# Linear attention and a maxout layer on one core: tiles of two pairs, held loads, maxima by block transposes, a new table

## The chip, the cores and the metric

The kernel runs on one core of a Trainium2 chip. The metric is the device time of one launch in microseconds (us). Three runs of the kernel before gave 290.2, 291.66 and 295.25 us; their median, 291.66 us, is the time before.

## The reference

Eight batches with eight heads each of 576 positions and 64 channels go through an attention with an exponential feature map, and the result goes through a maxout layer.

```python
def phi(x):
    proj = einsum('bhsd,df->bhsf', x, w_phi)                  # 64 -> 128 features
    proj = proj - max(abs(proj), axis=-1, keepdims=True)
    return concatenate([exp(proj), exp(-proj)], axis=-1)
q_p, k_p = phi(q), phi(k)
kv = einsum('bhsf,bhsd->bhfd', k_p, v)
z = sum(k_p, axis=2)
num = einsum('bhsf,bhfd->bhsd', q_p, kv)
den = einsum('bhsf,bhf->bhs', q_p, z)[..., None] + 1e-06
x = (num / den), heads side by side: 4608 tokens x 512
h = maximum(maximum(x @ w1, x @ w2), x @ w3)                   # 512 -> 768
out = h @ w_out                                                # 768 -> 512
```

## The kernel before

**Units and chunks.** The 64 heads are worked in 16 units of four heads, two pairs each (`attention(u)`). After two units one batch is complete, and `chunk(b, ...)` puts its first 512 positions through the maxout layer; the last 64 positions of all batches form chunk 8. The maxout is computed as w1 plus two maxima of differences, so a chunk has products "up" and "up2" (54 groups of each in all, four products of 512 columns a group, L700) and products "straight" and "down" into the output (L728, L733). The weights w2 - w1 and w3 - w1 are made by GpSimd and VectorE (L771), and w1 times w_out by TensorE once (transposes L783, products L797).

**One unit.** Tiles of 128 positions (two heads of 64) have q in partitions 0 to 63 and k in 64 to 127. Units 0 to 3 are brought into this form by TensorE transposes (L483, then a VectorE copy L486), the later ones by a DMA transpose (L498). Unit 0's q and k come in float32 through SyncE's queue in four loads, each of one pair of q or k (L441), and are cast (L445); units 1 to 3 come through GpSimd's software queue, which casts on the way (L452); the later ones come in float32 and are cast by GpSimd (L469). Products with w_phi follow (L521): for each tile one product for q on the upper 64 rows of the array and one for k on the lower 64 rows, side by side, in five groups of four or two tiles, into the banks psq and psk. VectorE takes the maxima of absolute values of both (L540), ScalarE the exponentials of k (L534).

The maxima of q have to be subtracted from the projections of q that have features in partitions. In units 0 and 1 that is done by products of the maxima with the negative identity (L602, L605). In the other 14 units TensorE transposes the maxima (L548), VectorE or ScalarE copies them (L552), and one DMA puts them into row 64 of the tiles (L556), over k, which has been used by then; one product of 65 rows on the whole array, with the weights `wphi_m` whose row 64 is -1, then gives the projection less the maximum (L600, five groups of 512, 512, 512, 512 and 256 columns). ScalarE takes both exponentials (L613). GpSimd scales v by the factors of k (em, L571, L575). 72 products of 64 rows, again side by side, form kv (L629), 40 products form numerator and denominator (L647), VectorE divides (L653, L654), and the unit's result is turned by TensorE (units 0 and 1, L667) or by a DMA transpose (L677).

**The order.** Every piece of work is a node. The order of all nodes, their engine and their PSUM bank or buffer are written out in a table, `PLAN`; a word like `15T1@5.6` says that node 15 goes to TensorE with bank 1, and is due at 5.6 us. Nothing waits for a due time: each engine runs its nodes in the order of the table, and waits only for the data and buffers that it needs. The due times come from a planner's costs, which are also written in the node (`{"PE": 0.87}`). The order binds within each engine's queue, GpSimd's and SyncE's queues of DMA issues among them. `fill` puts idle products (L828) where the table leaves gaps on TensorE.

```python
GROUPS = [(0, 4), (4, 4), (9, 4), (13, 4), (8, 2)]
a = nd("G", {"PE": 0.12 if n == 2 else 0.236 * len(part)}, ...)   # projections
a = nd("M", {"PE": 0.22 if n == 4 else 0.12}, mm, [n_v, n_phi], [qkT, psm, Eqb])
```

## Time and profile before

| what | value |
|---|---|
| median of three runs | 291.66 us |
| time of the profiled execution | 291.96 us |
| span of its profile, first to last instruction | 290.1 us |
| mean granted TensorE clock | 0.988 |
| TensorE busy (matmul) | 274.1 us |
| VectorE busy | 203.6 us |
| ScalarE busy | 199.4 us |
| GpSimd busy | 117.2 us |
| idle products of `fill` (L828) | 7.7 us |

The span is one profiled execution; 1.86 us lie outside it in the profiled time. A group of instructions in the page has a line of the kernel, an engine, an operation, the tiles it writes and reads, a count, the busy time and the mean of one. Matmuls are pipelined, so a product's own duration (379 ns for 512 columns) is longer than the step from its start to the next one's (0.22 us), and how long TensorE really takes for a group is read from starts. A busy share is a share of the stretch named; what a stage is bound by is read from the stretch, not from the whole.

### The profile page before, as it was taken

The page shows a single profiled execution, that of the slowest core. Times are in us where ns is not written, and L with a number is a line of the kernel's source. Part 1 is how long each engine was busy: PE and PEld are TensorE (multiplying, and loading weights), DVE is VectorE, ACT ScalarE, POOL GpSimd, SP SyncE. Part 2 cuts the span into 40 slices and gives each one's busy share as a digit, 9 for nine tenths or more (in the row PEclk, how much of TensorE's full clock was granted, in tenths as well). Part 3 has the DMA queues.
Part 4 walks back from the last instruction along what each step waited for, and adds up shares of the span by engine and source line. Part 5 has one row for each costly group of instructions (what it writes and reads, how often), then busy time and mean ns, then how long its engine had stood idle before and what let it go on. Part 6 is the DMA issues. An engine that isn't in the chain of part 4 may idle for free.

```text
span 290.1 us, 8530 instructions
## 1 busy us (share of the span) xinstructions
PE 274.1 (94%) x3526; PEld 154.6 (53%) x3563; DVE 203.6 (70%) x433; ACT 199.4 (69%) x455; POOL 117.2 (40%) x102
## 2 busy tenths in 40 slices
PE   8579989999999898999999999999999999999995
PEld 3347566455555554655556466465544654444443
DVE  3578898999898887797789869996673342156300
ACT  2579897899999877986797887889758420341021
POOL 8044889385746345836184535060606000000000
PEclk9897999999999999999999999999999999999999
DMA  7999979999998899999999991994620006370055
GB/s 173 276 251 209 283 157 263 231 281 217 226 186 307 169 273 197 291 276 241 205 263 224 274 285 35 163 183 87 144 49 0 2 3 127 70 168 18 0 129 163
DMA packets 68273, 51.48 MB, mean 177 GB/s; under 512 B 48778, under 2 KB 53002, under 8 KB 68234
## 3 DMA queue, kind: packets, MB, share of 16 engines
q1 hardware_dynamic: 63759, 45.55, 66.2%
q0 software_dynamic: 4000, 4.92, 9.8%
q8 instruction: 28, 0.46, 0.6%
q10 hardware_dynamic: 475, 0.46, 0.5%
q14 instruction: 11, 0.09, 0.1%
HBM read 34.67 MB, written 9.44 MB: 152 GB/s over the span
## 4 chain that ended last, share of the span: by engine, by line
PE 84%; DMA 10%; DVE 3%; issue 1%; POOL 1%; ACT 0%; POOLq 0%; DVEq 0%
PE ups L700 32%; PE ops L733 15%; PE ops L728 9%; PE psn L647 6%; PE kvps L629 6%; DMA w_bf<-in_moe_w_dram 6%; PE psq L521 5%; PE psm L600 5%; DMA xT<-x_sb 2%; DMA qkT<-mT 2%; PE pm L797 1%; PE tps L483 1%; DVE x_sb L654 1%; PE psm L602 1%; POOL qk_bf L452 1%
## 5 line engine op out<-in xcount | busy, mean ns | idle before, releaser
L700 PE MATMUL ups<-xT,w_bf 128*128 128x512 bf16 x414 | 100.5, 379 | 2.1 <-DMA xT<-x_sb 1.2
L534 ACT ACTIVATE Ek<-psk 128x512 bf16<-128x512 f32 (+1 forms) x160 | 81.6, 567 | 13.3 <-PE psk L521 6.9
L575 POOL TENSOR_TENSOR vab<-v_raw,em 128x1152 bf16<-128x1152 f32 (+1 forms) x36 | 68.2, 1907 | 49.8 <-ACT em L571 35.7
L613 ACT ACTIVATE Eq<-psm 128x512 bf16<-128x512 f32 (+1 forms) x160 | 80.2, 576 | 8.5 <-PE psm L600 7.3
L700 PEld LDWEIGHTS <-w_bf 128*128 128x128 bf16 x432 | 40.2, 98 | 45.9 <-issue 1.3
L540 DVE TENSOR_REDUCE mqp<-psq 128x4 bf16<-128x512 f32 (+1 forms) x80 | 48.9, 633 | 6.8 <-PE psk L521 5.9
L706 DVE TENSOR_TENSOR hT<-hT,ups 128x512 bf16<-128x512 bf16 x54 | 36.1, 682 | 24.0 <-PE ups L700 18.1
L540 DVE TENSOR_REDUCE mk<-psk 128x4 f32<-128x512 f32 (+1 forms) x80 | 49.3, 630 | 3.1 <-PE psk L521 1.7
L733 PE MATMUL ops<-wout_bf,hT 128*128 128x512 bf16 (+1 forms) x216 | 51.0, 373 | 0.4 <-issue 0.2
L741 ACT COPY osb<-ops 128x512 f32<-128x512 f32 (+1 forms) x24 | 13.7, 578 | 33.9 <-PE ops L733 27.4
L654 DVE TENSOR_TENSOR x_sb<-psn,rden 128x320 bf16<-128x320 f32 x64 | 31.5, 492 | 2.2
L733 PEld LDWEIGHTS <-hT 128*128 128x128 bf16 x222 | 21.0, 98 | 22.1
L708 ACT ACTIVATE hT<-ups 128x512 bf16<-128x512 f32 x36 | 21.7, 609 | 14.5 <-PE ups L700 13.6
L647 PEld LDWEIGHTS <-Eq 128*128 128x128 bf16 x640 | 25.4, 97 | 9.2
L647 PE MATMUL psn<-kv_sb,Eq 128*128 128x65 bf16 x640 | 27.8, 194 | 0.1
L521 PE MATMUL psq<-w,qkT 64*128 64x128 bf16 x288 | 25.3, 223 | 1.4 <-DVE qkT L486 0.7
L521 PE MATMUL psk<-w,qkT 64*128 64x128 bf16 x288 | 25.3, 224 | 0.0
L521 PEld LDWEIGHTS <-qkT 64*128 64x128 bf16 x576 | 17.1, 96 | 14.0 <-issue 10.4
L728 PE MATMUL ops<-xT 128*128 128x512 bf16 x88 | 24.1, 379 | 0.4
L600 PE MATMUL psm<-qkT,wphi_m 128*128 128x512 bf16 (+1 forms) x70 | 21.7, 358 | 1.4 <-DVE hT L706 0.8
L741 DVE COPY osb<-ops 128x512 f32<-128x512 f32 x13 | 8.9, 686 | 18.9 <-PE ops L733 16.1
L469 POOL CAST qk_bf<-k_raw 128x1152 bf16<-128x1152 f32 x12 | 14.1, 1185 | 18.2 <-DMA k_raw<-in_k_dram 13.0
(70 smaller groups left out, 232.0 us busy)
## 6 DMA issues: line engine op xcount, KB each, us to landing
v_raw<-in_v_dram SPq DMA_DIRECT2D x16, 576.0 KB, 5.2
out_dram<-osb SPq DMA_DIRECT2D x65, 128.0 KB, 2.5
q_raw<-in_q_dram SPq DMA_DIRECT2D x12, 576.0 KB
k_raw<-in_k_dram SPq DMA_DIRECT2D x12, 576.0 KB, 5.1
w_bf<-in_moe_w_dram POOLq DMA_DIRECT2D x3, 768.0 KB, 12.5
qk_bf<-in_k_dram POOLq DMA_DIRECT2D x3, 288.0 KB, 16.2
qk_bf<-in_q_dram POOLq DMA_DIRECT2D x3, 288.0 KB, 12.0
wout_bf<-in_moe_w_out_dram POOLq DMA_DIRECT2D x1, 768.0 KB, 21.1
```

Of the source, the lines that this page charges most:

```text
L521: nc.tensor.matmul(ps()[:, i, :], lhsT=cols[r, :], rhs=w2[r, c, :], start=True, stop=True)
L534: nc.scalar.activation(Ek[s]()[:, tiles_of(t0, n), :], of(1), EXP, scale=1.0 - 2.0 * s)
L540: nc.vector.tensor_reduce((mq, mk)[c]()[:, tiles_of(t0, n)], of(c), AXX, ALU.max, apply_absolute_value=True)
L575: (nc.vector if n_.eng == "DVE" else nc.gpsimd).tensor_tensor(vab()[:, g, t0:t1, 0:D], vb()[:, t0:t1, :], em()[:, g, t0:t1].unsqueeze(2).t ...
L600: nc.tensor.matmul(psm()[:, 0:w], lhsT=wphi_m, rhs=rhs, start=True, stop=True)
L613: nc.scalar.activation(Eqb()[s][:, cols], psm()[:, 0:w], EXP, scale=1.0 - 2.0 * s)
L647: nc.tensor.matmul(psn()[:, c, :], lhsT=Eqb()[g][:, t0:t0 + P], rhs=kv()[:, pr, ab, g, :], start=(g == 0), stop=(g == 1))
L654: nc.vector.tensor_tensor(x_sb()[:, pr, :, ab, :], psn()[:, :, 0:D], rden().to_broadcast([P, 5, D]), ALU.mult)
L700: nc.tensor.matmul(ups(), lhsT=w_bf[i + 1][:, ct, j * P:(j + 1) * P], rhs=tokens_of(ct), start=(ct == 0), stop=(ct == CT - 1))
L706: nc.vector.tensor_tensor(hT()[:, j, :], hT()[:, j, :], ups(), ALU.max)
L728: nc.tensor.matmul(ops_()[:, 0:width], lhsT=tile_of(ct, tt), rhs=line_w[c_i > MOVE][:, ct, cols], start=(ct == 0), stop=False)
L733: nc.tensor.matmul(ops_()[:, 0:width], lhsT=hT()[:, j, tt * P:(tt + 1) * P], rhs=wout_bf[:, j, cols], start=False, stop=(j == JT - 1))
```

## The change

Six things change together.

- **Tiles.** A tile now has one kind alone, q or k, with one pair of heads in partitions 0 to 63 and the other in 64 to 127. The two products of a tile, one on each half of the array's rows, go to two banks and belong to the two pairs. The five groups are: k and q tiles 0 to 3, k and q tiles 4 to 7, and tile 8 of both; the reductions and exponentials of the last group come in four pieces of 128 columns each instead of two of 256. For unit 0, where both pairs lie side by side in the cast copy, one transpose of 128 x 128 makes a tile instead of two.
- **Subtraction of the maxima.** VectorE turns the maxima by four 32 x 32 transposes, with no TensorE transpose and no copy out of PSUM. Two DMAs instead of one put them into rows 0 and 64 of the k tiles. The products of q are then two on each half: one with `w2`, one with `less`, whose rows 0 and 64 are -1 and whose other rows are zero. They are issued in two nodes per unit instead of five, the ninth tiles' products before the others of the first node and behind them in the second, and the second node's wait on a semaphore for the first node's.
- **Loads.** Unit 0's q and k come in pieces of four and five tiles of both pairs instead of one pair each, in the order k 4 to 8, q 4 to 8, k 0 to 3, q 0 to 3. GpSimd issues w1 first and unit 1's q behind it, and its next load, unit 1's k, waits behind a one-element copy that needs the first tiles of unit 0's q; all further GpSimd work stands behind it in its queue.
- **Groups of two.** The products of two banks can be split into halves that run side by side (`side_by_side`). The list `HALVED` chooses this for one group alone, numerator and denominator of the second pairs of unit 11; all others stay in full.
- **Nodes.** up, up2, straight and down come in pairs with the same products as before.
- **Table.** All 1498 nodes have a new place, 27 instead of 18 of the first maxout evacuations (L710) lie on VectorE, and all 28 DMAs of maxima are issued by SyncE (13 of 14 before).

```diff
--- before.py
+++ after.py
-GROUPS = [(0, 4), (4, 4), (9, 4), (13, 4), (8, 2)]
-BATCHES = [(0, 8), (9, 8), (8, 2)]
+GROUPS = [(1, 0, 4), (0, 0, 4), (1, 4, 4), (0, 4, 4), (None, 8, 1)]
+BATCHES = [(0, 0, 8), (1, 0, 8), (None, 8, 1)]
+FIRST = 1
+PIECES = [(1, 0, 4), (0, 0, 4), (1, 4, 4), (0, 4, 4), (None, 8, 1)]
 EW = UT * P + D
+TURN = 0.3
+TQ = 32
...
-2D0@0.8 4A@2.0 0G@0.5 6S0@0.7 3D@1.1 10S0@1.3 11D0@5.0 5D@5.5 7A@4.2 15T1@5.6 16D0@6.4 86D0@7.2 26T002300@7.2 29D@7.6 8S@1.9
...
+2D0@0.8 3D@1.1 12S0@0.7 13D0@4.2 8S0@1.2 9D@5.0 4A@2.0 5D@5.5 0G@0.5 19T1@4.9 23T2@5.7 24D0@6.2 21T3@5.8 20A@5.4
+35T004500@6.4 22D@6.5 45T67@6.6 47D@6.9 46D@7.2 10S@1.7 11A@6.0 15T1@6.8 16D@7.4 42T23@7.1 43D@7.7 6S@2.2 7A@6.6 17T1@7.9
...
+HALVED = """
+00000000000000000000000100000000000000000000000000000000000000000000000000000000000000000000000000000000000
...
+    ROWS = (slice(0, D), slice(D, P))
+
+    rows_done = tc.alloc_semaphore("rows_done")
+    turns = [0]
+
+    def half_full(ins):
+
+        turns[0] += 1
+        ins.then_inc(rows_done, 1)
+        tc.add_to_no_dep_group(f"turn{turns[0]}", ins.ins)
+        tc.no_tile_sem_insts.add(ins.ins.name)
+        return turns[0]
+
+    def behind(turn, product):
+
+        if not turn:
+            return product()
+        nc.tensor.wait_ge(rows_done, turn)
+        ins = product()
+        tc.declare_fence(ins.ins, group=f"turn{turn}")
+        return ins
+
+    halved, n_groups = [c == "1" for c in HALVED if c in "01"], [0]
+
+    def new_group():
+
+        n_groups[0] += 1
+        return n_groups[0] - 1, halved[n_groups[0] - 1]
+
+    def in_full(ps, steps, opens, closes):
+
+        for n, step in enumerate(steps):
+            out_, lhsT, rhs = step(ps, slice(0, P))
+            nc.tensor.matmul(out_, lhsT=lhsT, rhs=rhs, start=opens and n == 0, stop=closes and n == len(steps) - 1)
+
+    def side_by_side(state, steps, opens, closes, turn=None, turns_after=True):
+
+        for n, step in enumerate(steps):
+            for half in ((0, 1), (1, 0))[state]:
+                i = half ^ state
+                out_, lhsT, rhs = step(i, ROWS[half])
+                ins = behind(turn, lambda: nc.tensor.matmul(out_, lhsT=lhsT, rhs=rhs, start=opens and n == 0,
+                                                            stop=closes and n == len(steps) - 1))
+                turn = None
+        return half_full(ins) if turns_after and not closes else None
...
-    w2 = const.tile([P, 2, DF], BF16, name="w2")
-    wphi_m = const.tile([P, DF], BF16, name="wphi_m")
+    w2 = const.tile([P, DF], BF16, name="w2")
+    less = const.tile([P, DF], BF16, name="less")
...
+        nc.vector.memset(less, 0.0)
+        for p0 in (0, D):
+            nc.vector.memset(less[p0:p0 + 1, :], -1.0)
...
+            if what < 2 and u == 0:
                 mains.append(None)
+                for c0, c1 in ((0, 4), (4, NT)):
+                    def main(what=what, c0=c0, c1=c1, raw=raw):
+                        nc.sync.dma_start(by_pairs(raw())[:, :, c0 * D:c1 * D], rows_of(what, 0, 0, 2)[:, :, c0 * D:c1 * D])
+                    n_ = nd("const", {"SP": 0.5}, main, [], [raw], pipe=1.6 * (c1 - c0) / NT, lat=1.7, packet=PACKET)
+
+                    def to_bf16(n_, what=what, c0=c0, c1=c1, raw=raw):
+                        copy_on[n_.eng](half_of(what, c0, c1), by_pair(raw())[:, :, c0:c1, :])
+                    n_ = nd("C", {"DVE": 0.1 + 0.09 * (c1 - c0), "ACT": 0.2 + 0.1 * (c1 - c0)}, None, [n_], [raw, qk])
+                    n_.fn = lambda n_=n_, f=to_bf16: f(n_)
+                    cast.append((what, c0, c1, n_))
+            elif what < 2 and by_pe:
+                mains.append(None)
+
+                def main(what=what):
+                    nc.gpsimd.dma_start(by_pairs(qk()[:, what]), rows_of(what, u, 0, 2))
+                deps = []
+                if u == 1 and what == FIRST:
+                    deps = [nd("gate", {"POOL": 0.1}, lambda: nc.gpsimd.tensor_copy(
+                        qk()[0:1, FIRST, 0, 0:1], raw_bufs(0)[0]()[0:1, 0, 0:1]), [n_ for w_, c0, c1, n_ in units[0]["loads"] if w_ == 0 and c0 == 0],
+                        [raw_bufs(0)[0], qk])]
+                cast.append((what, 0, NT, nd("L", {"POOL": 0.85}, main, deps, [qk], pipe=1.8, lat=2.1, packet=PACKET_BF)))
...
+                def tp(tiles=tiles, tps=tps):
+                    for i, (w_, c) in enumerate(tiles):
+                        if not raw_form:
+                            nc.tensor.transpose(tps()[:, i, :], qk()[:, w_ * NT + c, :], ident)
+                            continue
+                        for pr in range(2):
+                            nc.tensor.transpose(tps()[ROWS[pr], i, :], qk()[:, w_, pr * NT + c, :], ident)
...
+        for what, c0, n in GROUPS:
+            ps = [bank("psp", [P, 4, DF]) for _ in range(2)]
+            tail = what is None
+
+
+            def proj(what=what, c0=c0, n=n, ps=ps, tail=tail):
+                for i in range(2 if tail else n):
+                    for half in range(2):
+                        t = i * NT + c0 if tail else what * NT + c0 + i
+                        nc.tensor.matmul(ps[half]()[:, i, :], lhsT=qkT()[ROWS[half], t * P:(t + 1) * P], rhs=w2[ROWS[half], :],
+                                         start=True, stop=True)
+            a = nd("G", {"PE": 0.11 if tail else 0.22}, proj, [tr[x] for x in tiles_of(what, c0, n)] + [n_phi],
+                   [qkT, mk, mq] + ps + Ek, mode=1)
+            if what != 0:
+                projs.append(a)
+            for w_, i in [(w_, i) for w_ in ((0, 1) if tail else (what,)) for i in range(2)]:
+                to = slice(i * NT + c0, i * NT + c0 + n)
+                of = slice(w_, w_ + 1) if tail else slice(0, n)
+
+                def red(w_=w_, i=i, to=to, of=of, ps=ps):
+                    nc.vector.tensor_reduce((mq, mk)[w_]()[:, to], ps[i]()[:, of, :], AXX, ALU.max, apply_absolute_value=True)
+
+                def ex(s, i=i, to=to, of=of, ps=ps):
+                    nc.scalar.activation(Ek[s]()[:, to, :], ps[i]()[:, of, :], EXP, scale=1.0 - 2.0 * s)
+                for s in range(2 if w_ else 0):
+                    exps.append(nd("ek", {"ACT": 0.49 if n == 4 else 0.24}, lambda s=s, ex=ex: ex(s), [a],
+                                   [ps[i], Ek[s]], locks=[ps[i]]))
+                n_ = nd("r", {"DVE": 0.607 if n == 4 else 0.22}, red, [a, n_const], [ps[i], (mq, mk)[w_]], locks=[ps[i]])
+                reds[w_].append((n_, (i,)))
...
-            pmT = bank("pmT", [P, P], BF16)
-            n_r = nd("R", {"PE": 0.06}, lambda: nc.tensor.transpose(pmT(), mq(), ident), reds[0::2], [mq, pmT])
-            mT = buf("mT", 2, [UT, P], BF16)
-
-            def do_mT(n_):
-                copy_on[n_.eng](mT(), pmT()[0:UT, :])
-            n_mt = nd("mT", {"ACT": 0.25, "DVE": 0.2}, None, [n_r], [pmT, mT], locks=[pmT])
-            n_mt.fn = lambda: do_mT(n_mt)
-            n_v = nd("V", {"ACT": 0.7, "SP": 0.7}, None, [n_mt] + projs, [mT, qkT], lat=2.2, pipe=0.1)
-            n_v.fn = lambda: queue_of[n_v.eng].dma_start(
-                qkT()[D:D + 1, :].rearrange("o (t c) -> o t c", c=P), mT())
+            mT = buf("mT", 2, [TQ, P + TQ], BF16)
+
+            def across():
+                for g in range(P // TQ):
+                    nc.vector.transpose(mT()[:, g * TQ:(g + 1) * TQ], mq()[g * TQ:(g + 1) * TQ, :])
+            n_r = nd("R", {"DVE": 0.35}, across, q_reds, [mq, mT])
+            n_v = []
+            for pr in range(2):
+                def row(n_, pr=pr):
+                    queue_of[n_.eng].dma_start(qkT()[pr * D:pr * D + 1, NT * P:UT * P].rearrange("o (c i) -> o c i", i=P),
+                                               mT()[pr * NT:(pr + 1) * NT, 0:P])
+                n_ = nd("V", {"ACT": 0.65, "SP": 0.6}, None, [n_r] + projs, [mT, qkT], lat=2.2, pipe=0.1)
+                n_.fn = lambda n_=n_, f=row: f(n_)
+                n_v.append(n_)
...
-                    nc.tensor.matmul(psm()[:, 0:w], lhsT=wphi_m, rhs=rhs, start=True, stop=True)
...
+        eqs = {}
+        pst, done, a = bank("psm", [P, 2, P]), {}, None
+        for ab in range(2):
+            ch = ROWS[ab]
+            psm = [bank("psm", [P, 8, D]) for _ in range(2)]
+
+            def mm(ab=ab, ch=ch, psm=psm):
+                def main(w, t0, pr, **kw):
+                    return nc.tensor.matmul(psm[pr](), lhsT=w[ROWS[pr], :], rhs=tiled(qkT())[ROWS[pr], t0:t0 + NT - 1, ch], **kw)
+
+                def last(w, t, start, stop):
+                    kw = dict(start=start and not ab, stop=stop and bool(ab))
+                    return nc.tensor.matmul(pst()[:, ab, :], lhsT=w[ROWS[ab], :], rhs=tiled(qkT())[ROWS[ab], t, :], **kw)
+                parts = ((w2, 0, dict(start=True, stop=False)), (less, NT, dict(start=False, stop=True)))[0:2 - by_product]
+                for w, t0, kw in parts if not ab else ():
+                    ins = last(w, t0 + NT - 1, **kw)
+                if not ab:
+                    done[0] = half_full(ins)
+                for w, t0, kw in parts:
+                    for pr in ((0, 1), (1, 0))[ab]:
+                        main(w, t0, pr, **kw)
+                turn = done[0]
+                for w, t0, kw in parts if ab else ():
+                    behind(turn, lambda: last(w, t0 + NT - 1, **kw))
+                    turn = None
+                if by_product:
+                    for pr in range(2):
+                        for c in range(NT - 1):
+                            nc.tensor.matmul(psm[pr]()[:, c, :], lhsT=mq()[:, pr * NT + c:pr * NT + c + 1].to_broadcast([P, P]),
+                                             rhs=minus[:, ch], start=False, stop=c == NT - 2)
+                    for pr in range(2 * ab):
+                        nc.tensor.matmul(pst()[:, pr, :], lhsT=mq()[:, pr * NT + NT - 1:(pr + 1) * NT].to_broadcast([P, P]),
+                                         rhs=minus, start=False, stop=pr == 1)
+            cost = (0.49, 0.49) if not by_product else (0.86, 0.98)
+            a = nd("M", {"PE": cost[ab]}, mm, [n_phi] + (q_reds + [n_minus] if by_product else n_v) + ([a] if a else []),
+                   [qkT, Eqb, pst] + psm + ([mq] if by_product else []), mode=1)
...
+            psn, done = [bank("psn", [P, 5, W]) for _ in range(2)], {}
+
+            g_, half = new_group()
+
+            def nmm(state, pr=pr, psn=psn, done=done, half=half):
+                def step(c, g):
+                    def of(ab, r):
+                        t0 = (8 * pr + 4 * ab + c if c < 4 else MT + pr) * P + (D if c == 4 and ab else 0)
+                        return psn[ab]()[:, c, :], Eqb()[g][r, t0:t0 + P], kv()[r, pr, ab, g, :]
+                    return of
+                if half:
+                    done[state] = side_by_side(state, [step(c, g) for c in range(5) for g in range(2)], not state, bool(state), done.get(0))
+                else:
+                    for c in range(5):
+                        in_full(state, [step(c, g) for g in range(2)], True, True)
+            two = []
+            for state in range(2):
+                two.append(nd("N", {"PE": 0.3 if half else 0.312}, lambda state=state, f=nmm: f(state),
+                              (two if half else []) + (n_kvs if half else [n_kvs[state]]) + (eqs[pr, 0] + eqs[pr, 1] if half else eqs[pr, state])
+                              + eqs[False], [Eqb, kv, x_sb] + (psn if half else [psn[state]]), mode=int(half),
+                              hold=TURN if half and state else None, group=g_))
```

642 lines of the change are left out of this document (307 added, 335 removed).

## Prediction

> **What bounds the kernel now.** I read the busy times first, then the same by stretches of the span, then the starts of single products on TensorE, last the waits and the shapes on VectorE.
>
> ```profile
> PE 274.1 (94%) x3526; PEld 154.6 (53%) x3563; DVE 203.6 (70%) x433; ACT 199.4 (69%) x455; POOL 117.2 (40%) x102
> PEclk9897999999999999999999999999999999999999
> ```
>
> TensorE is busy nearly all the time at full clock, except at the start. By stretches (busy us of each engine, count in brackets, then clock, DMA share, GB/s):
>
> ```profile
> 10.00:20.00 10.00, 7.77 (x116) 4.48 (x116) 7.88 (x15) 8.77 (x20) 1.97 (x3) 0.83 1.13 272
> 20.00:30.00 10.00, 9.21 (x191) 7.15 (x193) 7.70 (x14) 8.00 (x21) 5.25 (x7) 0.83 1.21 208
> 30.00:110.00 80.00, 76.42 (x1223) 45.27 (x1233) 72.14 (x157) 70.69 (x166) 51.77 (x41) 1.00 0.99 237
> 110.00:215.00 105.00, 102.55 (x1421) 59.11 (x1437) 85.83 (x184) 86.54 (x200) 46.65 (x34) 1.00 0.88 198
> 215.00:290.00 75.00, 71.36 (x538) 35.83 (x543) 26.48 (x50) 22.82 (x48) 5.62 (x6) 1.00 0.28 66
> ```
>
> From 30 us on TensorE idles 9.6 of 260 us, and the last 3.6 of these are mostly the tail. So a microsecond of work added to TensorE there is nearly a microsecond of time, and one taken away likewise. VectorE is at 90% between 30 and 110 us, ScalarE at 88%: room, but little. Before 30 us TensorE waits for loads:
>
> ```profile
> PE tps L483 <- ACT qk_bf L445: 2.5, 2, 1.3
> PE pwT L783 <- DMA w_bf<-in_moe_w_dram: 1.8, 1, 1.8
> ```
>
> Unit 0's second halves of q and k are cast only at 8.71 and 10.26 us, and w1 lands at 20.57. Everything below is added to the profiled execution, 291.96 us (span 290.1), which lies 0.3 above the median 291.66. A measurement can tell about 2% (5.8 us) from no change.
>
> **TensorE, products.** The view of starts shows what a product of half the rows costs, and what a change between half and full rows costs.
>
> ```profile
> 119.97 0.22 PE L521 MATMUL psq<-w,qkT 64*128 64x128 bf16 x1
> 119.97 0.22 PE L521 MATMUL psk<-w,qkT 64*128 64x128 bf16 x1
> 120.03 0.22 PE L521 MATMUL psq<-w,qkT 64*128 64x128 bf16 x1
> 120.03 0.22 PE L521 MATMUL psk<-w,qkT 64*128 64x128 bf16 x1
> 120.18 2.76 PE L700 MATMUL ups<-xT,w_bf 128*128 128x512 bf16 x12
> 122.88 0.23 PE L521 MATMUL psq<-w,qkT 64*128 64x128 bf16 x1
> ```
>
> A pair of half products starts together and is followed by the next pair 0.06 us later. After the last pair the next product, on all rows, starts 0.15 us later: 0.10 lost. I took all such changes after 30 us, from start to start, less the columns at 128 in 0.053 us: 33 into half rows lose 0.099 in the median, 33 out of them 0.095, while 210 changes between groups of full rows lose 0.003. Now the orders: with the projections and kv as the only half groups the old table has 65 changes after the start stage (66 are in the trace). In the new one the subtraction is a half group as well, and with the one halved group there are 96. 31 x 0.10 = **+3.1 us**.
>
> The subtraction's columns: before 4 x 512 + 256 = 2304 a unit on all rows, 0.96 us. After, two products for each 512, side by side in pairs: 4 x 2 x 512 / 2 = 2048 columns of time, plus the ninth tiles, 2 x 2 x 128, on one half alone. If products start in order, as the pairs above do, nothing runs beside these 512 and a unit takes 1.07 us, 0.107 more; if the other half runs past them, 0.96 and nothing. 14 units: 0 to +1.5; I take **+1.5**, since every start in the view is in order. The Trainium skill, page TensorEngine Tiling (Array Packing), section Key Properties, says that tiles operate independently; by that the term would be 0 and the sum 294.3. The trace shows independence only for neighbours in order.
>
> The transpose of the maxima goes: 14 x 0.06 (start 41.67, next product 41.73) = **-0.8**. The projections (36 products a unit), kv, divisions and the maxout groups keep their products: 0. The halved group has as many columns in pairs; its wait for its own first half, and the like wait in each second subtraction node, stand in TensorE's queue ahead of all later products: 0 for the latter, as eight half products lie between, at most the 0.22 of one product's duration for the former. In units 0 and 1 the subtraction loses columns, and unit 0 loses 18 transposes (about 0.5 us); both lie where TensorE waits anyway: 0, or -1.
>
> **VectorE and ScalarE.** Rows by shape:
>
> ```profile
> L540 DVE TENSOR_REDUCE mqp<-psq 128x4 bf16<-128x512 f32 x64 | 42.8, 686 | 6.5 <-PE psk L521 5.6 <-PE psq L521 0.5
> L540 DVE TENSOR_REDUCE mqp<-psq 128x2 bf16<-128x256 f32 x16 | 6.8, 422 | 0.4 <-PE psk L521 0.4
> L552 DVE COPY mT<-pmT 18x128 bf16<-18x128 bf16 x8 | 1.6, 206 | 1.9 <-PE pmT L548 1.9
> ```
>
> From 512 to 256 columns a reduction loses 0.264 us, so one of 128 costs about 0.29, or 0.23 behind another (neighbours overlap by some 0.055). 64 x 0.23 in place of 32 x 0.37 is +2.9. Four 32 x 32 transposes do not occur before; VectorE's smallest rows are 0.11 (memset) to 0.21 (the copy above), less overlap 0.055 to 0.155, so 14 x 4 gives 3.1 to 8.7; I take 0.13, near the 1x1 cast (0.135), +7.3. The copies save 1.6; nine more maxout evacuations at 0.63 add 5.7, and take 5 from ScalarE, to which 64 short exponentials in place of 32 add about as much (0.404 for 256 columns, 0.61 for 512). VectorE in sum: +14, from 10 to 16. About 6 of it fall between 30 and 110 us: 72.1 + 6 = 78 of 80. The fullest 10 us now hold 9.84 (50 to 60 us), so VectorE becomes level with TensorE there. I charge **+1.5**: 78 at 96% need 81.5 us. The bounds are 0 (other engines' waits give way) and the second rival below.
>
> **DMA queues.** SyncE issues 28 DMAs of maxima for 13, at 0.81 us each now (0.78 to 1.08); 14 more cost it some 9 us, hidden as SyncE mostly waits (single waits up to 28 us). Behind them stand loads and transposing DMAs; without cover a unit's tiles come 0.7 later. The bytes stay.
>
> **Start.** GpSimd's first five issues now stand between 1.42 and 6 us. The packets show that its software queue works in order, from 4.0 us on, and that it shares with SyncE's one to one: 387 to 383 packets between 4 and 10 us. After the change w1 and unit 1's q fill that queue at once, so the held loads (unit 1's k, unit 2, w_out) would not have run earlier anyway, and unit 0's last piece still comes near 10.3: before it 1180 KB have to pass, about 600 of them after 4 us. Behind GpSimd's wait stand these loads and its work on v; none is needed before about 18 us. What changes is w1: first in the queue, its 512 packets of 0.134 us, alternating with pieces of 1 to 1.3 KB (0.047 for 1 KB), end near 10.5 instead of 20.6. The wait of 1.8 us goes; next late is unit 0's q. I take **-1.5**; bounds -4.3 (both waits above) and +1 (q later, since the pieces have half the bytes and the rival packets are larger).
>
> **Sum:** 291.96 + 3.1 + 1.5 - 0.8 + 1.5 - 1.5 = 295.8 us, 1.4% above the median. With the terms at their bounds (6.9 for VectorE, from the second rival): 289.0 to 303.7.
>
> **Rivals.**
> - *The hold does nothing.* The start term is then 0, as w1 only changes places with q and k of unit 1 and something else is late: 297.3. For it: one to one sharing. The Trainium skill, page DMA: Bandwidth & Descriptors, section Queues, rings and completion order, has each engine go round between rows packet by packet; then one load in GpSimd's queue takes the same turns as six, and the trace agrees (387 to 383). Against it: w1's place.
> - *VectorE becomes the bound.* It is at 90% between 30 and 110 us and never over 98%. If 90% is all that this order of waits allows, 78.4 us need 86.9: +6.9 for +1.5, 301.2. It decides once VectorE's added work in that stretch exceeds 0.9 x 80 - 72, which is nothing. For it: 9.6 us of VectorE's idle time end with a reduction, most of them waits for products, so the two engines wait for each other. Against it: 50 to 60 us.
> - *Unit 1's k is late.* The hold opens near 10.5, issue 0.8. The first software load now takes 7.0 us to its last packet (18.3), w1 17.0. The order wants it at about 19.4 (due 15.9, and the start runs 3.5 late). If it takes 10.7, everything moves by 2.6: 298.4. Decides beyond 8 us.
> - *Faster.* The order of waits improves with w1 early and TensorE's idle between 30 and 110 us (3.6) goes; changes of rows hide in waits of others: 291.96 - 0.8 - 4.3 - 3.6 = 283.3. For it: the clock was halved twice (0.83 in two stretches) and w1's wait lies ahead of the second. Against it: TensorE's work rises.
>
> **Numbers.** Forecast 0.36, hold without effect 0.10 (both within 2%, 0.46); VectorE 0.26 and late k 0.12 (slower, 0.38); faster 0.16. The range from 286.5 to 302 leaves out most of the fast case (about 0.12) and the top of the slow one (0.08).
>
> **What would show it.** Changes of rows: starts of the new subtraction products 0.15 behind a full product; span of TensorE after 30 us. Subtraction: 1.07 or 0.96 us a unit. VectorE: 0.13 for a transpose, over 95% between 30 and 110 us. Start: no wait of L783 for w1, first exponentials still near 10.8 us. I am wrong if TensorE gains idle time beyond 12 us after 30, or if the first kv comes over 3 us earlier or later than 28.0.

## The result and the profile after

The changed kernel takes 298.88 us in the median of four runs (297.9 to 300.0) where the kernel before takes 291.69: ratio 1.027, 95% interval 1.020 to 1.033. A second measurement, beside runs 5 and 6 below, gave 299.8 against 290.4 us, ratio 1.031 (1.026 to 1.036). So it is slower by 2.5 to 3%; I use 1.029, the middle of the two, to compare with. (Ratios leave out executions that took over 1.5% longer than the fastest of the same kernel; in the third move of run 7 these are three of six, so its median and its ratio do not match.) The profiled execution is 298.36 us long, span 296.6, 6.4 more than the one before.

From the page of the changed kernel, the busy times and the granted clock in 40 slices:

```profile
PE 279.2 (94%) x3658; PEld 157.3 (53%) x3658; DVE 220.8 (74%) x524; ACT 195.7 (66%) x470; POOL 117.7 (40%) x104
PEclk9879999999999999999999999999999999999999
```

TensorE is as full as before in sum. VectorE has gained 17.2 us, of which 9.0 lie behind 215 us, where it has room: it is busy there for 35.45 of 81.6 us, for 26.48 of 75 before. The view by stretches of the changed kernel (busy us of PE, PEld, DVE, ACT and POOL, then clock, DMA share, GB/s):

```profile
10.00:20.00 10.00, 7.40 (x77) 4.58 (x77) 5.37 (x12) 7.35 (x18) 3.47 (x6) 0.66 1.10 200
20.00:30.00 10.00, 8.87 (x217) 6.36 (x215) 9.91 (x22) 10.00 (x29) 7.81 (x11) 1.00 0.84 162
30.00:110.00 80.00, 74.10 (x1225) 44.02 (x1222) 74.60 (x181) 67.76 (x170) 49.46 (x39) 1.00 1.00 243
40.00:64.00 24.00, 18.88 (x275) 10.68 (x275) 21.51 (x47) 17.40 (x44) 21.05 (x15) 1.00 0.88 243
110.00:215.00 105.00, 103.85 (x1499) 59.01 (x1498) 91.27 (x226) 86.68 (x212) 47.47 (x35) 1.00 0.86 197
```

Two things differ from before. Between 30 and 110 us TensorE is busy for 74.1 us, 2.3 fewer than before, and more than all of that lies between 40 and 64 us: 18.9 there, where the kernel before has this:

```profile
40.00:64.00 24.00, 22.55 (x295) 12.88 (x297) 22.29 (x47) 20.50 (x49) 17.68 (x12) 1.00 0.86 238
```

And from 110 to 215 us TensorE is full (103.85 of 105). The waits of TensorE in the changed kernel say what opened the hole (total, times, longest; the first row lies in the start):

```profile
PE tps L547 <- ACT qk_bf L501: 4.4, 2, 2.8
PE kvps L710 <- POOL vab L641: 2.2, 2, 1.9
PE ups L381 <- DVE mqp L597: 1.4, 1, 1.4
```

The wait for w1 is gone, as forecast. A wait for GpSimd's multiplication of unit 2's v (L641) is new; so is one for VectorE's maxima (near 59 us). The chain of the changed kernel leads from that wait back to a load (start, length):

```profile
34.37 0.05 DVE v_raw L519
...
34.44 8.46 DMA v_raw<-in_v_dram
...
43.04 0.11 POOL vab L641
43.15 1.97 issue
45.12 2.13 POOL vab L641
...
47.29 1.24 PE kvps L710 x70
...
57.37 2.18 DVE w_bf L900
59.55 0.61 DVE mqp L597
```

VectorE's gate copy (a one-element copy that the load waits for) ran at 34.4 us, behind reductions and divisions in VectorE's queue. Unit 2's load of v took 8.5 us, GpSimd's two multiplications 4.2 (the "issue" of 1.97 is the first of them), and TensorE stood from 45.4 to 47.3. From 48.7 to 62.8 us the chain runs through VectorE alone, and 5.0 us of it are the three differences of weights (L900).

How the loss builds up is seen best against the table: the lag of an instruction is its start less its due time. The median over all reductions, exponentials, divisions and maxout evacuations due in ten microseconds:

| due from | before | changed | difference |
|---|---|---|---|
| 30 us | 6.5 | 5.7 | -0.8 |
| 40 us | 8.3 | 8.9 | 0.7 |
| 60 us | 8.9 | 12.2 | 3.3 |
| 150 us | 11.9 | 15.8 | 3.9 |
| 250 us | 12.2 | 16.6 | 4.4 |

The new table itself ends 2.1 us later (its last TensorE node at 276.45 against 274.35), and 2.1 + 4.4 are the 6.5 us of the span. A start that is 0.8 better is followed by 4.1 us lost between 30 and 60 us, and by a slow leak of 1.1 us after that. In the second profiled execution of the changed kernel the lag is 6.3 us at 30, 12.5 at 60 and 16.8 at 250: the start is only 0.3 better there, and 3.8 us are lost between 30 and 60 us.

### The profile page after: what moved, and what is told of

It reads as the page before. It is cut to its first block, busy times and chain, and to the rows that moved or that the text cites. A ratio compares the mean times of both kernels' runs of the same rounds, so it can differ in the third digit from the quotient of the medians.

```text
span 296.6 us, 8888 instructions
## 1 busy us (share of the span) xinstructions
PE 279.2 (94%) x3658; PEld 157.3 (53%) x3658; DVE 220.8 (74%) x524; ACT 195.7 (66%) x470; POOL 117.7 (40%) x104
## 4 chain that ended last, share of the span: by engine, by line
PE 71%; DVE 12%; DMA 10%; ACT 3%; issue 1%; POOL 1%; SPq 0%; DVEq 0%; POOLq 0%
PE ups L381 28%; PE ops L381 23%; PE kvps L710 5%; PE psn L381 5%; PE psp L586 4%; DMA xT<-x_sb 4%; PE psm L662 4%; DVE mqp L597 3%; DMA q_raw<-in_q_dram 3%; DVE mk L597 3%; DMA v_raw<-in_v_dram 3%; DVE w_bf L900 2%; ACT Ek L600 1%; ACT Eq L694 1%; DVE qkT L553 1%
## 5 line engine op out<-in xcount | busy, mean ns | idle before, releaser
L600 ACT ACTIVATE Ek<-psp 128x512 bf16<-128x512 f32 (+1 forms) x192 | 83.5, 520 | 11.8 <-PE psp L586 7.0
L641 POOL TENSOR_TENSOR vab<-v_raw,em 128x1152 bf16<-128x1152 f32 (+1 forms) x36 | 68.5, 1918 | 43.9 <-ACT em L637 29.3
L694 ACT ACTIVATE Eq<-psm 128x512 bf16<-128x512 f32 (+1 forms) x160 | 77.3, 584 | 5.8 <-PE psm L662 4.7
L597 DVE TENSOR_REDUCE mqp<-psp 128x4 bf16<-128x512 f32 (+1 forms) x96 | 50.0, 551 | 8.9 <-PE psp L586 6.6
L597 DVE TENSOR_REDUCE mk<-psp 128x4 f32<-128x512 f32 (+1 forms) x96 | 49.8, 547 | 7.2 <-ACT Ek L600 4.1
L809 DVE TENSOR_TENSOR hT<-hT,ups 128x512 bf16<-128x512 bf16 x54 | 35.7, 682 | 11.5 <-PE ups L381 9.8
L811 ACT ACTIVATE hT<-ups 128x512 bf16<-128x512 f32 x27 | 16.0, 614 | 21.3 <-PE ups L381 21.1
L586 PE MATMUL psp<-w,qkT 64*128 64x128 bf16 x576 | 27.0, 220 | 1.5 <-DVE qkT L553 0.9
L586 PEld LDWEIGHTS <-qkT 64*128 64x128 bf16 x576 | 18.2, 95 | 17.0 <-issue 11.5
L813 DVE TENSOR_SCALAR hT<-ups 128x512 bf16<-128x512 f32 x27 | 18.3, 685 | 7.1 <-PE ups L381 7.1
L710 PE MATMUL kvps<-vab,Ek 64*128 64x65 bf16 x1152 | 20.6, 190 | 2.6 <-POOL vab L641 2.2
L870 DVE COPY osb<-ops 128x512 f32<-128x512 f32 (+1 forms) x14 | 8.7, 628 | 18.9 <-PE ops L381 14.6
L710 PEld LDWEIGHTS <-Ek 64*128 64x128 bf16 x1152 | 19.1, 94 | 5.3 <-issue 3.2
## 6 DMA issues: line engine op xcount, KB each, us to landing
w_bf<-in_moe_w_dram POOLq DMA_DIRECT2D x3, 768.0 KB, 12.5
```

Of the source, the lines that this page charges most:

```text
L586: nc.tensor.matmul(ps[half]()[:, i, :], lhsT=qkT()[ROWS[half], t * P:(t + 1) * P], rhs=w2[ROWS[half], :], start=True, stop=True)
L597: nc.vector.tensor_reduce((mq, mk)[w_]()[:, to], ps[i]()[:, of, :], AXX, ALU.max, apply_absolute_value=True)
L600: nc.scalar.activation(Ek[s]()[:, to, :], ps[i]()[:, of, :], EXP, scale=1.0 - 2.0 * s)
L641: (nc.vector if n_.eng == "DVE" else nc.gpsimd).tensor_tensor(vab()[:, g, t0:t1, 0:D], vb()[:, t0:t1, :], em()[:, g, t0:t1].unsqueeze(2).t ...
L694: nc.scalar.activation(Eqb()[s][:, to:to + w], ps().rearrange("p a b -> p (a b)"), EXP, scale=1.0 - 2.0 * s)
L710: nc.tensor.matmul(kvps[ab]()[:, t // NT, g, :], lhsT=Ek[g]()[r, t, :], rhs=vab()[r, g, t, :], start=(t + g == 0), stop=(t == UT - 1 and g ...
```

## The experiments

Three theories. A: VectorE's added work is what comes back in the time. B: the hole from 45 to 47 us, with what feeds it, does. C: the added changes between half and full rows do, all along the span. Some edits change a due time in the table and leave the word where it is: the program sorts the nodes by their due times before it issues them, so that the due time sets the place in an engine's queue.

**1. No hold.** The copy that holds GpSimd's queue does nothing.

```diff
-deps = [nd("gate", {"POOL": 0.1}, lambda: nc.gpsimd.tensor_copy(
-    qk()[0:1, FIRST, 0, 0:1], raw_bufs(0)[0]()[0:1, 0, 0:1]), ...
+deps = [nd("gate", {"POOL": 0.1}, lambda: None, ...
```

> The changed kernel with the copy that holds GpSimd's queue left out, so that unit 1's k is asked for as soon as w1 is; the rest is as in the changed kernel (298.9 us, 1.027 of the kernel before). Theory: the hold is what lets unit 0's q in, and the first block of scores, at 26.1 us in the changed kernel against 27.95 before, comes back by 0.5 to 1.5 us; part of that reaches the end: 299.3 to 300.4 us. Rival, the hold does nothing, since q's last piece came at 11.7 us with it and at 10.3 us in the kernel before, which had none: 298.3 to 299.5 us with the first exponentials still near 12.2 us. Third: the hold itself costs, because unit 1's k starts at 11.7 us: below 298 us.

Measured: 299.96 us, ratio 1.033 (1.026 to 1.040), against 1.029. First exponentials at 11.5 us, first K at 25.98 (26.10 with the hold). The time is in the range of the first theory, but its mechanism was not seen, since the first K came no later. No effect of the hold is shown, though the interval leaves room for 3 us; the better start is not its work.

**2. Unit 2's v earlier.** Gate and load moved ahead of unit 5's q and k on SyncE's queue.

```diff
-... 166D2@28.7 ... 167S@28.9
+... 166D2@18.95 ... 167S@19.3
```

> The changed kernel with one VectorE copy (the gate of unit 2's v) and its load put ahead in their queues, from 28.7 us of the table to 18.95 us. In the changed kernel that copy ran at 34.4 us, the load landed at 42.9 us, GpSimd's multiplication with v ran 43.0 to 47.25 us, and TensorE's K products started at 47.3 us behind a wait of 2 us; before, the load was asked for at 30.4 us. Theory B (the late load of unit 2 made the slot between 40 and 60 us late, and the time never came back): GpSimd's multiplication starts 3 to 4 us earlier, the wait at 45 us goes, and of the other waits between 50 and 60 us (2.8 us) half: 295 to 297 us. Rival A (VectorE's added work makes that slot late): the wait at 45 us goes, but the waits on VectorE at 52 to 59 us grow by as much: 298 to 299.3 us. Theory C (the added changes between half-row and full-row products, spread over the whole span): no more than 0.5 us from 298.9 us.

Measured: 300.51 us, ratio 1.035 (1.029 to 1.041). A miss for B in this form: K of unit 2 came at 48.35 us instead of 45.22, not earlier. The chain of this kernel shows why:

```profile
26.84 12.84 DMA q_raw<-in_q_dram
...
39.82 1.14 POOL qk_bf L526
```

Unit 5's q now came behind v; its cast stands ahead of the multiplication in GpSimd's queue, so that began at 46.2 us instead of 43.0. One late load was changed for another.

**3. No differences on VectorE.** w3 minus w1 is left out.

```diff
-n_.fn = lambda n_=n_, f=diff: f(n_)
+n_.fn = (lambda: None) if i else lambda n_=n_, f=diff: f(n_)
```

> The changed kernel without VectorE's three differences of weights (w3 minus w1 is left out, w3 is used as it is loaded; 5.3 us of VectorE between 47 and 54 us in the changed kernel, 2.6 us before). Theory A (VectorE is the bound between 30 and 110 us): the waits of TensorE for VectorE at 53.7 us (0.7) and 58.4 us (1.6) and part of the lag that VectorE has built up go: 295 to 297 us. Theory B: the wait for v at 45 us comes before and stays: 297.5 to 299 us. Theory C: 298.4 to 299.4 us.

Measured: 295.94 us, ratio 1.019 (1.010 to 1.028), about 2.9 us less than the changed kernel, in A's range; the interval overlaps that of the changed kernel. The hole at 45 us stayed, as B says, with K's rest at 47.08 us; the wait for VectorE's maxima near 59 us went. With the differences went TensorE's own wait for them (0.5 us), too. In the profiled executions the lag at 250 us is 1.7 less than in the changed kernel, of which 0.65 was there at 30 us, ahead of any difference.

**4. One block turned.** Of the four 32 x 32 transposes of a unit one is left.

```diff
-for g in range(P // TQ):
+for g in range(1):
     nc.vector.transpose(mT()[:, g * TQ:(g + 1) * TQ], mq()[g * TQ:(g + 1) * TQ, :])
```

> The changed kernel with one of the four 32x32 transposes of the maxima in each unit; the other three quarters of the maxima are ones, so part of the by-product is left out, and the two transfers of the row are as before. 42 transposes at 0.2 us go, 8.7 us of VectorE, about 3.2 us of it between 30 and 110 us. Theory A (VectorE is the bound there): 295.5 to 297.5 us, with VectorE's lag behind the table between 50 and 110 us less by 2 to 3 us. Theories B and C: 298.3 to 299.4 us, VectorE only shows more idle time.

Measured: 298.18 us, ratio 1.028 (1.020 to 1.036). No gain is shown, against A, but the interval still holds a gain of 2.5 us, and the profiled run had a longer hole (K's first products at 46.0 us, the rest at 48.1, at half clock). So VectorE's load could not be priced in this kernel. The next two runs price the added work in the kernel before.

**5. VectorE's transposes in the kernel before.** Beside the copy of the maxima, four transposes of a constant that nobody reads.

```diff
 copy_on[n_.eng](mT(), pmT()[0:UT, :])
+for g in range(4):
+    nc.vector.transpose(scr_o[:, g * 32:(g + 1) * 32], minus[g * 32:(g + 1) * 32, 0:32])
```

> The kernel before with four 32x32 transposes on VectorE added in each of 14 units, of a constant tile into a tile that nobody reads, beside the copy of the maxima: 56 at 0.2 us, 11.6 us of VectorE, about 4.3 us of it between 30 and 110 us. Theory A (added VectorE work between 30 and 110 us comes back in the time): 294.5 to 297 us where the kernel before takes 291.7, ratio 1.009 to 1.018. Rival (VectorE has room for it, since it is idle for 8.5 us between 30 and 110 us and TensorE runs at its own pace): under 1.004.

Measured: ratio 1.0098 (1.0060 to 1.0136), 2.9 us. Their row in this kernel:

```profile
L555 DVE STREAM_TRANSPOSE scr_o<-minus 32x32 bf16<-32x32 bf16 x56 | 11.1, 198 | 0.7
```

11.1 us on VectorE cost 2.9 us of time (1.7 to 4.0), about a quarter; all but some 1.4 us of the work lies ahead of 215 us. Theory A holds for the kernel before.

**6. Changes of rows in the kernel before.** A product of 64 rows and 16 columns ahead of two of the five by-product products, in a bank that is then overwritten.

```diff
+if hd in (0, 2):
+    nc.tensor.matmul(psm()[:, 0:16], lhsT=w2[0:D, 0, :], rhs=rhs[0:D, 0, 0:16], start=True, stop=True)
 nc.tensor.matmul(psm()[:, 0:w], lhsT=wphi_m, rhs=rhs, start=True, stop=True)
```

> The kernel before with a product of 64 rows and 16 columns put ahead of two of the five products for the by-product in each of 14 units (28 small products of 7 ns each, into a bank that the next product overwrites): each adds a change from full rows to half rows and back, up to 56 changes, fewer where the product ahead of it has 64 rows already. Theory C (a change costs TensorE 0.10 us wherever it falls): 28 to 56 changes, plus 2.8 to 5.6 us: 294.5 to 297.3 us, ratio 1.010 to 1.020. Rival (the changes fall into waits that are there anyway): under 1 us, ratio under 1.004.

Measured: ratio 1.0133 (1.0084 to 1.0181), 3.9 us. In its trace 60 changes into half rows and 60 out of them follow 30 us, where the kernel before has 33 and 33; they lose 12.7 us together instead of 7.25. So 54 changes lose 0.10 us each on TensorE, and 0.07 (0.045 to 0.10) in the time. C holds for the kernel before as well.

**7. Where the hole comes from.** The rates of the DMA queues from 20 to 60 us, one number for each microsecond, of the kernel before, and then of the changed one:

```profile
GB/s 203 208 207 207 206 206 209 212 217 204 203 170 298 377 364 355 278 253 233 230 164 57 5 0 37 115 334 410 410 403 207 26 253 235 184 362 399 205 131 348
```

```profile
GB/s 204 215 201 94 7 21 145 341 249 147 189 237 268 289 253 283 284 277 284 293 290 249 210 212 166 158 290 123 295 385 412 383 399 389 406 279 323 387 297 92
```

From 23 to 27 us the changed kernel's queues run dry: 94, 7, 21 and 145 GB/s where the kernel before moves some 207. SyncE's next loads (unit 1's v, unit 5's q and k) stand behind a VectorE copy that ran at 24.8 us, and GpSimd's (unit 3's q and k, w2, w3) behind unit 0's multiplications with v, until 25.2 us. What was not moved then crowds the queues until 43 us: GpSimd waits 1.6 us for unit 5's q and 2.0 for its k, and v lands at 42.9. An empty stretch need not harm: the kernel before has one from 41 to 45 us (57, 5, 0 and 37 GB/s), and TensorE waits for no load between it and 70 us. Three moves follow from that. First, w2's load ahead of unit 0's multiplications:

```diff
-59G0@14.5 ... 1097G@20.5
+1097G@14.3 59G0@14.5 ...
```

> The changed kernel with one load moved in GpSimd's queue: that of w2 (768 KB) ahead of unit 0's multiplications with v instead of behind them. In the changed kernel the DMA queues moved 7 KB from 24 to 26 us (402 KB in the kernel before), since SyncE's next loads stood behind a copy of VectorE that ran at 24.8 us and GpSimd's behind the multiplications (25.2 us); the loads left over then crowd 27 to 43 us, unit 5's q and k come 1.6 and 2.0 us late for GpSimd's casts and unit 2's v at 42.9 us, and TensorE stands from 45.2 to 47.2 us. Putting v ahead in SyncE's queue did not help (its load then took 16.4 us). Theory B3 (the empty stretch of the queues is the cause): the 768 KB fill it, unit 5's k and unit 2's v land 2 to 3.5 us earlier, K starts before 46 us, the hole falls under 0.8 us: ratio to the kernel before 1.014 to 1.022, 295 to 297.5 us. Rival (VectorE's lag sets that slot anyway): unchanged at 1.026 to 1.032.

Measured: 297.34 us, ratio 1.026 (1.022 to 1.030). The stretch is filled (209 GB/s from 24 to 26 us, where the changed kernel has 14), unit 5's k is cast at 38.5 us instead of 39.2, but v's gate still ran at 33.8 us, v landed at 42.9 and the hole stayed: the rival's outcome. With w3's load moved too:

```diff
-59G0@14.5 ... 1097G@20.5 ... 1098G@22.1
+1097G@14.3 1098G@14.4 59G0@14.5 ...
```

> As the kernel before this one, with w3's load (768 KB) moved as well, behind w2's. Theory B3: 1.5 MB are more than the empty stretch holds (some 700 KB at 200 KB per us), so unit 3's q and k, behind them on GpSimd's queue, come later, but the stretch from 27 to 43 us is lighter by as much; K starts before 45.5 us: ratio 1.012 to 1.022. Rival: unchanged at 1.026 to 1.032, or longer if unit 3's q and k become what TensorE waits for.

Measured: 297.50 us, ratio 1.028 (1.024 to 1.032), no better: GpSimd stood idle for 7 us ahead of unit 1's multiplications, which began at 33.1 us, and the one for unit 2 began at 42.6 us. Then v behind unit 5's k on SyncE's queue, with v's gate copy on VectorE (node 166) due at 18.95 instead of 28.7 us, and with GpSimd's first difference of w2 behind the multiplication:

```diff
-166D2@28.7 ... 371S1@20.4 ... 167S@28.9 ... 1100G@32.0 ... 1102G@38.6
+166D2@18.95 ... 371S1@20.4 167S@20.5 ... 1100G@38.55 1102G@38.6
```

> The changed kernel with two orders altered: unit 2's load of v is asked for right behind unit 5's q and k (20.5 us of the table instead of 28.7 us; putting it ahead of them, an earlier run, made unit 5's q late and cost 4 us more of waiting), and on GpSimd unit 2's multiplication with v stands ahead of the first difference of w2 (2.1 us) instead of behind it. Theory B2 (GpSimd's order, not VectorE's load, made the hole of TensorE between 44 and 47 us, and the half clock that follows such a hole in some runs): the multiplication starts near 41 us instead of 43.0 us, K near 45.2 us instead of 47.3 us, the hole shrinks to under 0.5 us: 294.5 to 297 us. Theory A (VectorE is the bound there): the hole closes but the next wait on VectorE (58.8 to 60.2 us) grows: 298 to 299.5 us. Theory C (the changes of rows spread over the whole span): 298.3 to 299.3 us.

Measured: 298.8 us in the median of six executions, from 295.1 to 303.0. The ratio of 1.020 (1.013 to 1.026) is that of the three that took 295.1 to 297.1 us; the median of all six is within 1 us of the 299.8 that the changed kernel takes beside it. In the profiled execution, the longest of the six, v was asked for at 28.2 us and landed at 44.6, 16.4 us later; the hole is there. So B2 is not shown. The changed kernel run beside it:

> The changed kernel itself once more, unaltered, beside the three that follow, so that they share a chip and their runs of the kernel before: 297.5 to 300.5 us, 1.02 to 1.035 of the kernel before. If the wait of TensorE at 45 us (2 us in the profiled run) is what makes its times spread, runs with a lower mean granted clock are the longer ones.

Measured: 299.8 us, ratio 1.031 (1.026 to 1.036). Its six runs bear out the spread only in part: those with a clock of 0.971 took 299.8, 300.3 and 301.4 us, those with 0.983 to 0.989 took 298.1, 298.5 and 299.8.

**8. The three moves together.**

> The changed kernel with the three moves together that did not close the hole alone: w2's load ahead of unit 0's multiplications on GpSimd's queue, unit 2's v asked for right behind unit 5's k on SyncE's, and GpSimd's first difference of w2 behind unit 2's multiplication with v. Each of them alone left something else in front of that multiplication: the first the gate of v (landed 42.9 us), the second and third together the crowded queues (v landed at 44.6 us). Theory B (one chain through GpSimd, v's load and TensorE's K makes the hole from 45 to 47 us and the half clock behind it): v lands by 41 us, the multiplication starts by 41.2 us, K by 45.5 us, the hole is under 0.5 us, the granted clock between 40 and 64 us is 1.00: ratio to the kernel before 1.012 to 1.021. Rival (the time is set by VectorE's and TensorE's added work, and the hole only takes what the later waits give back): 1.024 to 1.031, with the wait on VectorE's maxima near 59 us as long as before or longer.

The gate copy of v is due at 18.95 us here, too.

Measured: 296.44 us (295.8 to 297.2), ratio 1.0192 (1.0159 to 1.0226), 0.7 to 1.2% below the two measurements of the changed kernel; the interval lies below that of the second and overlaps that of the first. Views of this kernel, the rates of the queues as above, then the stretch from 40 to 64 us, then TensorE's waits between 30 and 70 us:

```profile
GB/s 216 195 205 205 216 207 210 282 347 313 278 283 278 301 283 285 300 263 236 221 220 100 135 291 138 309 383 398 413 396 406 397 154 32 0 25 226 399 403 127
```

```profile
40.00:64.00 24.00, 20.85 (x347) 12.47 (x348) 23.42 (x51) 19.49 (x51) 21.78 (x14) 1.00 0.79 225
```

```profile
PE ups L381 <- POOL w_bf L900: 1.2, 2, 0.7
PE ups L381 <- DVE mqp L597: 1.1, 1, 1.1
...
PE kvps L710 <- POOL vab L641: 0.2, 1, 0.2
```

There is no empty stretch between 23 and 27 us, the multiplication starts at 41.28 us, K at 45.17 with the rest at 45.53: the wait for v is 0.2 us. The lag at 60 us is 9.9 instead of 12.2, at 250 us 14.05 instead of 16.6, so 2.5 us of the 4.4 went with the three moves. They have a price, the first row of the waits: TensorE waits 1.2 us for the differences that GpSimd now makes later. What limits that slot next is read from the second view: VectorE is busy for 23.4 of 24 us, and TensorE still waits 1.1 us for its maxima, for 1.4 before the moves. That points to A, once B is out of the way; no run takes VectorE's work out of this kernel.

**9. w1 first in the kernel before.**

```diff
-85G1@1.1 84G@1.9 ... 1075G@3.2
+1075G@1.05 85G1@1.1 84G@1.9 ...
```

> The kernel before with one load moved: w1 first in GpSimd's queue, ahead of unit 1's q and k, as the changed kernel has it (there is no hold). Theory of the start term: TensorE's wait for w1 near 13 us (1.8 us) goes and the first block of scores comes 1 to 1.5 us earlier: 290.2 to 290.9 us where the kernel before takes 291.7, ratio 0.995 to 0.998. Rival (unit 1's q and k, now behind 768 KB, come 3 us late and take the gain): 1.000 to 1.010. Rival (unit 0's last q is what the start waits for, whatever is ahead of it): 0.999 to 1.002.

Measured: 294.59 us, ratio 1.020 (1.014 to 1.026), slower by some 5 to 6 us. A miss for the first theory; the second was right in kind and small by half. TensorE's waits in this kernel begin with

```profile
PE tps L483 <- DMA qk_bf<-in_q_dram: 5.7, 1, 5.7
PE tps L483 <- ACT qk_bf L445: 2.5, 2, 1.6
```

The wait for w1 is gone, and unit 1's q is 5.7 us late in its place; the first K starts at 33.54 us, for 27.95. No version beat the kernel before; the nearest, the three moves, is still 1.9% slower.

## Why the prediction was right and wrong

The time lies in the range and 3.1 us above the forecast; the likeliest case was "within 2%", and it came out just slower. So the number held, but not by the sum as it was written: one term came to almost nothing, VectorE's was too small, and a loss that the sum does not have fills the difference. Step by step:

- **Changes of rows, +3.1: right in kind, a little large.** The trace has 98 changes after 30 us (49 in, 49 out), forecast 96, with medians of 0.099 and 0.095 us. Without three that fall into longer waits they lose 9.70 us instead of 7.25, +2.45. Run 6, in the kernel before, shows such changes in the time at about 0.07 us each, so some 2 us.
- **Columns of the subtraction, +1.5: wrong, it is 0.4 at most.** The view of starts in the changed kernel:

```profile
56.47 0.23 PE L666 MATMUL psm<-qkT,w 64*128 64x128 bf16 x1
56.48 0.39 PE L662 MATMUL psm<-qkT,w 64*128 64x512 bf16 x1
56.54 0.22 PE L666 MATMUL psm<-qkT,less 64*128 64x128 bf16 x1
56.60 0.38 PE L662 MATMUL psm<-qkT,w 64*128 64x512 bf16 x1
```

  The ninth tile's product starts at 56.47 us on one half, the long one on the other half at 56.48, and the next short one at 56.54, when its own half is free. By the program the long product at 56.48 is the fourth of the node: it started ahead of the second and third, which wait for the first half. The twelve products of two adjacent nodes, to the start of the projections at 57.46, take 0.99 us, for the 0.96 that the prediction has for the kernel before. Seven times a node stands alone and products on full rows follow: it takes about 0.64 us, of which 0.10 are the change of rows, and that is 0.06 more than half of 0.96. Seven times 0.06 are 0.4 us, an estimate. I had taken the other end because all earlier starts were in pairs. The rule of the Trainium skill that I weighed there (TensorEngine Tiling (Array Packing), Key Properties: tiles operate independently) is what this trace shows.
- **The transpose of the maxima, -0.8: right in kind.** The 14 products are gone from the trace, and nothing else took their place on TensorE; no run shows their worth by itself.
- **VectorE, +1.5: the mechanism right, the size wrong.** Its work grew by 17.2 us, forecast 14, for a plain reason: a 32 x 32 transpose takes 0.198 us, one starting 0.207 after the other, where I took 0.13, the price of a one-element copy. My bound of 8.7 us for all was passed too. The table was made with the same fault: it plans 0.35 us for the four transposes of a unit (`{"DVE": 0.35}`), which take 0.82.

```profile
L614 DVE STREAM_TRANSPOSE mT<-mqp 32x32 bf16<-32x32 bf16 x56 | 11.1, 198 | 0.7
```

  By run 5 a microsecond on VectorE costs 0.26 of time, so 17.2 would be 4.5, and the 8.2 that lie ahead of 215 us would be 2.1; both are estimates from the kernel before, and in the changed kernel only run 3 shows a part of it (2.9 us for 5.3 of work between 50 and 60 us). Between 30 and 110 us, from which I took the charge, VectorE came to 74.6 us and not to 78; with the hole closed it is 77.0. Another 2.7 us of its work came from the three differences, which took twice as long in this execution (last section); the other parts of my 14 came out 3 to 4 us smaller together.
- **Start, -1.5: about half of it or less.** The first K came 1.85 us earlier (26.10; 1.3 in the second run), but the lag at 30 us is only 0.8 better, 0.3 in the second run. Packets of w1 started until 12.7 us, not 10.5, unit 0's last piece was cast at 11.69 us, not 10.3, and the first exponentials came at 12.21, not 10.8. Run 9 shows that the change of places of w1 with unit 1's q and k is not free in itself: in the kernel before it costs 5 to 6 us.
- **What failed most** is a step that is not in the sum. Under "Start" I followed the held loads up to "none is needed before about 18 us", and under "DMA queues" counted issues and bytes; the order of the loads between 19 and 43 us, new in the table, I never walked through. There SyncE's and GpSimd's loads both stand behind something that ends at 25 us. The three moves of run 8, which close the hole, are worth 2.2 to 3.4 us (1.027 or 1.031 less 1.019); which part of it is the empty stretch, the crowd behind it or GpSimd's order stays open, since no smaller move closed the hole.

The terms, 2 for the changes, 0 to 0.4, -0.8, 2 to 4.5 for VectorE, 2.8 for the hole and -0.8 for the start, add up to some 5 to 8 us, for a measured 7.2 and 9.4. This is a sum of estimates and not a proof: VectorE's term is the loosest, since run 4 did not show its part, the prices of VectorE and of the changes are those of the kernel before, and VectorE's work and the hole act on the same stretch.

Of the rivals, *VectorE becomes the bound* gave the right side and 301.2 us, but not its sign: VectorE is at 93% between 30 and 110 us, not over 95; only with the hole closed does it come to 96% there (98% from 40 to 64 us). *The hold does nothing* agrees with run 1 as far as its interval goes, though it is not why the start term fell. *Unit 1's k is late* did not happen: unit 5's k and unit 2's v were late, for the same sort of reason. *Faster* fell with TensorE's added idle time between 40 and 64 us. My own signs of being wrong, idle time beyond 12 us after 30 us and the first K over 3 us away, did not come: 10.5 us and 1.85. A hole in one place and fuller work later cancel in such a sum.

## What to carry to other kernels

When a table is redrawn, walk every DMA queue in its new order and ask, for each stretch, which instruction must have ended before the next load can be issued; a sum of bytes or of issues does not show a queue that runs dry. Here the stall was not one late load: each smaller move that was tried only handed the wait to what stood next in GpSimd's queue or on the crowded transfers. And what a microsecond on an engine that is 90% busy costs can be measured by adding work that nobody reads, before a change is built on it.

## What was not expected of the hardware

**VectorE's differences wait for GpSimd.** Three subtractions of the same shape, before and in the changed kernel:

```profile
L771 DVE TENSOR_TENSOR w_bf<-w_bf 128x1024 bf16<-128x1024 bf16 x3 | 2.6, 859 | 0.0
```

```profile
L900 DVE TENSOR_TENSOR w_bf<-w_bf 128x1024 bf16<-128x1024 bf16 x3 | 5.3, 1756 | 0.0
```

In the changed kernel the slowest, 2.26 us, started at 57.3 us, while GpSimd worked on unit 3's v from 56.9 us, and those GpSimd multiplications took 4.64 us for two instead of 4.20. The Trainium skill, page SBUF — State Buffer, section "SBUF: two separate sides", says that VectorE, for an operation with two SBUF inputs, and GpSimd, for one that reads SBUF, lock a shared pair of ports for a whole instruction. The rows agree, and all traces of this case more closely: of 34 differences that started during a GpSimd instruction, 32 ended 0.54 to 0.55 us after it, and the five that started beside none took 0.67 to 0.69 us. A GpSimd instruction that came next at once took 0.45 to 0.5 us longer. So how long a difference takes depends on what GpSimd has begun just before: the three took 5.3 us in this execution and 4.0 (0.72, 0.94 and 2.33) in the second one of the same kernel. That moving them apart would gain time was not tried.

**The clock after a short hole.** After the hole the granted clock was halved in some executions and not in others. One microsecond a line, without the differences (run 3) and in the changed kernel:

```profile
46.00:47.00 1.00, 0.00 (x0) 0.00 (x0) 0.00 (x0) 0.28 (x1) 1.00 (x2) 0.54 1.57 263
47.00:48.00 1.00, 0.92 (x35) 0.92 (x36) 0.00 (x0) 0.00 (x0) 1.00 (x2) 0.50 0.56 157
```

```profile
46.00:47.00 1.00, 0.00 (x0) 0.00 (x0) 0.38 (x1) 0.64 (x2) 1.00 (x1) 1.00 1.28 290
47.00:48.00 1.00, 0.71 (x47) 0.71 (x48) 0.00 (x0) 0.00 (x0) 1.00 (x2) 1.00 0.92 123
```

In the first it was halved from 46.1 to 52.9 us, 6.8 us behind a stretch of 1.9 us without matmuls; in the second run of the changed kernel it was halved for 3.4 us. The traces show what decides. In all 14 the clock changes only on a grid of 3.41 us. Between 30 and 285 us there are eight cells of this grid at full clock in which TensorE stood without matmuls for 1.50 us or more in sum (1.50 to 3.2): each is followed by half clock. In every other cell at full clock it stood for 1.48 us or less, and full clock follows. In the changed kernel's profiled execution a border of the grid, at 46.2 us, cuts the hole: 1.26 us of standing lie in the cell ahead of it, 1.06 in the cell behind, and the clock stays. In run 3 the border at 46.1 us has 1.50 us ahead of it. What the half clock costs is not shown: the changed kernel's lag at 60 us is 12.2 with full clock, and 12.5 in the second run, which was 0.5 behind at 30 us already. The Trainium skill, page TensorE: Matmul & The Clock Gate, Part 1, lets the clock fall after an idle window of about 3.4 us that runs freely. The grid fits a window that runs freely; but a cell with 1.5 us of standing was enough here, so that the window need not be idle throughout, and the measurement decides.
